# Tiles 0 and 1 centred first and scaled at their eviction, with the first statistics moved behind the low parts of the weights

## The chip, the cores and the metric

The kernel runs on one NeuronCore of one Trainium2 chip. The profile names five engines: PE (matrix multiplication; PEld is its loading of the stationary operand), DVE (the vector engine), ACT (the scalar engine), POOL (GpSimd) and SP, which here only issues DMAs. Each engine works through its own list of instructions in order, and waits on semaphores for the others. The metric is the device time of one execution in microseconds (us). Three runs of the kernel before gave 485.28, 485.30 and 487.21 us, a median of 485.3.

## The reference, cut to what matters

The input x has 2048 rows of 512 elements. Every row is normalised (mean taken off, divided by the root of its variance plus 1e-5). The result xn goes two ways: through q, k, v and a local dilated attention (32 heads of 16, a window of 8 keys at a distance of 2), and through a squared-ReLU network with 1792 hidden units. The product of the two is added to x.

```python
xn = _layernorm(x, axis=-1)            # (x - mean) / sqrt(var + 1e-5)
qkv = xn @ wqkv                        # 512 -> 3 * 512
# per position and head: softmax over 8 keys q.k / 4, then the weighted sum of v
s = attention(qkv) @ wo
h = xn @ w1 + b1
g = silu(relu(h)**2 @ w2 + b2)
return x + s * g
```

For a row with mean m and r = 1 / sqrt(var + 1e-5), xn @ w equals ((x - m) @ w) * r: the factor r may be applied to the row before the product or after it.

## The kernel before, in words

The 2048 rows are 16 tiles of 128 rows, and four chunks of four tiles. Precision is kept by splitting: each fp32 operand becomes a high part (ACT copies it to the type fp32r: `high`) and a low part (DVE or POOL takes the high part off the fp32 value: `low`; `split` does both), and a product is three matmuls, high by high, high by low and low by high (`PASSES`). A product of one tile with 512 columns is thus 12 matmuls of 128x512.

The work has two phases. In the first, q, k and v of all tiles are made and stored to DRAM (`sq`, `sk`, `sv`), from where the attention reads them back; tiles 2 to 15 go in pairs, most of them with a scheme that saves one product in eight by sums of the operands (the tiles `S`, made from `Sf`). In the second, the network runs chunk by chunk (`up`: 14 groups of 128 hidden units, PSUM tile `ph`; `down`: accumulated in `pb`), the attention on DVE runs beside it, and its result is multiplied by `wo` (`pw`). For chunk 0, `up` reads the transposed tiles 0 to 3 from one SBUF tile, `xT`; its first two groups are computed inside the last pair (a = 14) of the first phase.

Before a tile can be multiplied it goes through: a load of x (`load_x`), statistics on DVE (`stats`: BN_STATS, BN_AGGR into `mv`, and `rs` = variance + 1e-5), a power of -0.5 on POOL (`rs` again, in `moments`), the normalisation on DVE (`norm`: one TENSOR_SCALAR that subtracts the mean and multiplies by `rs`, into `xn`), a transpose on PE into PSUM (`pxT`), and the split into `xT` (`high` on ACT, `low` on DVE). The very first product, k of tile 0, takes no split: `x0` (`xT0f`) and the raw weights `wqraw` are multiplied in fp32, so that it can begin before the weights have been split. 18 transposes of the identity (`WARM`, tile `warm`) keep PE busy until then.

`evacuate` copies a product from PSUM into a staging tile `stg` (ACT, `AF.Copy`), and `store_qkv` sends a pair of tiles to DRAM through SP.

What sets the order: every compute call goes through `Ordered`, which keeps the order of the Python code on its engine; `queue` does the same for SP's DMAs. From pair 2 on, a table `plan` says behind which product (pair a, step 0 to 5) a function is called: `at(a, step, f, ...)`. Two running clocks, one of PE and one of DVE, add up an assumed price of each instruction and decide where the attention's instructions are put in; they are set to fixed values once (`clock.update`).

Of the kernel before, what the change touches and what calls it, by code (L numbers as in the profile page):

```python
# [9 lines left out]
F32 = mybir.dt.float32  # L10
FR = mybir.dt.float32r
AF = mybir.ActivationFunctionType
OP = mybir.AluOpType
AX = mybir.AxisListType

P = 128
S = 2048
D = 512
F = 1792
KT = D // P  # L20
# [11 lines left out]
GR = 8  # L32
# [11 lines left out]
SEVEN = range(4, 16, 2)  # L44
VSEVEN = range(6, 14, 2)

WARM = 18
WARM2 = 3

TURN = 4  # L50
# [9 lines left out]
def body(ctx: ExitStack, tc: tile.TileContext, x, wqkv, wo, w1, b1, w2, b2, out):  # L60
# [34 lines left out]
    PE, V, A, G = Ordered(nc.tensor, "PE"), Ordered(nc.vector, "V"), Ordered(nc.scalar), Ordered(nc.gpsimd)  # L95

    def not_before(t):
        clock["V"] = max(clock["V"], t)
# [3 lines left out]
    def queue(out, in_):  # L102

        tc.keep_in_program_order(dma(out, in_))

    const = ctx.enter_context(tc.tile_pool(name="const", bufs=1))
    dram = ctx.enter_context(tc.tile_pool(name="dram", bufs=1, space=bass.MemoryType.DRAM))
# [7 lines left out]
    def psA(name):  # L115
        return psum.tile([P, 512], F32, name=name, tag="acc", bufs=4)
# [4 lines left out]
    def psT(name):  # L121
        return psum.tile([P, 512], F32, name=name, tag="tp", bufs=2)
# [16 lines left out]
    xins = {}  # L139
# [3 lines left out]
    warm = psA("warm")  # L143
    for n in range(WARM):
        PE.transpose(warm[:, :P], ident, ident)
# [3 lines left out]
    def tile_rows(a, t):  # L149
        return a[t // 2 * UP:(t // 2 + 1) * UP, :].rearrange("(p e) d -> e p d", e=2)[t % 2]  # L150

    def load_x(t):
        xins[t] = px.tile([P, D], F32, name=f"x{t}", tag="x", bufs=4)
        queue(xins[t], tile_rows(x, t))
# [38 lines left out]
    mhalf = const.tile([P, 1], F32, name="mhalf")  # L193
# [3 lines left out]
    def constants():  # L197
# [5 lines left out]
        for w in range(W - 1):  # L203
            G.memset(mask[:GR, :(W - 1 - w) * DIL, w], -1e9)

    b1t = const.tile([P, NF], F32, name="b1t")
    b2t = const.tile([P, D], F32, name="b2t")

    sq = dram.tile([GR, S, CH], F32, name="sq")
    sk = dram.tile([GR, HALO + S, CH], F32, name="sk")  # L210
    sv = dram.tile([GR, HALO + S, CH], F32, name="sv")
# [15 lines left out]
    def load_u(what, u):  # L227
        n = BI if what == "q" else WIN
        src = dict(q=sq, k=sk, v=sv)[what]

        t = att.tile([P, n, CH], F32, name=f"{what}{u}", tag="k" if (what, u) == ("v", NU - 1) else what)
        row = src[0, u * UP:u * UP + 1, :]
        ap = bass.AP(tensor=row.tensor, offset=row.offset, ap=[[BI * CH, NB], [src.shape[1] * CH, GR], [1, n * CH]])
        A.dma_start(t.rearrange("p i c -> p (i c)"), ap)
        return t
# [20 lines left out]
    def start(n, u):  # L256
        tiles[n, u] = load_u(n, u)
        landing[n, u] = clock["PE"] + LOAD
# [161 lines left out]
    mv, means, rs, shifts, xn, xb, pTs, xt, xT, seen, Sf, Sp, xts = ({} for _ in range(13))  # L420

    def moments(t, st):
        mv[t] = px.tile([P, 2], F32, name=f"mv{t}", tag="mv", bufs=2)
        rs[t] = px.tile([P, 1], F32, name=f"rs{t}", tag="rs", bufs=4)
        V.bn_aggr(mv[t], st)
        V.tensor_scalar_add(rs[t], mv[t][:, 1:2], 1e-5)
        G.tensor_tensor(rs[t], rs[t], mhalf, op=OP.pow)
# [14 lines left out]
    def stats(t):  # L442
        st = px.tile([P, 6], F32, name=f"st{t}", tag="st", bufs=2)
        V.bn_stats(st, xins[t])
        moments(t, st)

    def norm(t):

        src = xins.pop(t)
        if t < TURN:  # L450
            xn[t] = dst = px.tile([P, 2, D], F32, name=f"xn{t}", tag="xb", bufs=2)[:, 0]
        else:
            if t % 2 == 0:
                xn[t] = px.tile([P, 4, 2, P], F32, name=f"xn{t}", tag="xn", bufs=2)
            dst = xn[t // 2 * 2][:, :, t % 2].rearrange("p a (k c) -> p k a c", k=KT)
            src = src.rearrange("p (k a c) -> p k a c", a=4, k=KT)
        if t < STATS:
            halves = [slice(0, D // 2), slice(D // 2, D)] if t == 0 else [slice(None)]
            for i in halves:
                V.tensor_scalar(dst[:, i], src[:, i], mv[t][:, 0:1], rs[t], op0=OP.subtract, op1=OP.mult)  # L460
        else:
            A.activation(dst, src, AF.Identity, bias=shifts.pop(t), scale=rs[t])
        if t < 2:
            load_x(t + 4)

    def place(t):
        if t < TPC:
            parts = xT[0][:, :, t]
        else:
            parts = xts[t] = pxT.tile([P, KT, 2, P], FR, name=f"xt{t}", tag="xt", bufs=4)  # L470
        xt[t] = parts.rearrange("p k a n -> p a k n")
# [95 lines left out]
    def qkv(t, s, between=None, late=False, new=True):  # L567

        ps = psA(f"pq{t}_{s}")
        order = [(kt, a, b) for kt in range(KT) for a, b in PASSES]  # L570
        if late:
            order.sort(key=lambda o: o[1])
        for n, (kt, a, b) in enumerate(order):
            PE.matmul(ps, xt[t][:, a, kt], wq[2 * s + kt // 2][:, b, kt % 2, :], start=n == 0, stop=n == 11,
                      skip_group_check=True)
            if between and n == 5:
                between()
        evacuate(t, s, ps, new)

    def evacuate(t, s, ps, new=True):  # L580
        if t % 2 == 0 and new:
            new_stg(t, s)
        A.activation(stgs[s][:, :, t % 2], ps.rearrange("p (g c) -> p g c", g=GR), AF.Copy)
        if t % 2:
            store_qkv(t, s)

# [42 lines left out]
    def highs(s, kt):  # L629
        for i in (kt, kt + 1):  # L630
            high(*wq_parts(s, i))

    def lows(s, kt):
        low(*wq_parts(s, kt), V)
        low(*wq_parts(s, kt + 1), V)


    stats(0)
    high(*wq_parts(1, 0))
    norm(0)  # L640
    xT[0] = xTa.tile([P, KT, TPC, 2, P], FR, name="xT0", tag="xT")
    place(0)
    pT = [psT(f"pxT0_{kt}") for kt in (0, 2)]
    for kt in range(KT):
        PE.transpose(pT[kt // 2][:, kt * P:(kt + 1) * P], xn[0][:, kt * P:(kt + 1) * P], ident)
    stats(1)
    low(*wq_parts(1, 0), V)

    x0 = hpool.tile([P, D], F32, name="xT0f", tag="h", bufs=4)
    for kt in (0, 2):  # L650
        cols = slice(kt * P, (kt + 2) * P)
        A.activation(x0[:, cols], pT[kt // 2][:, cols], AF.Copy)
    norm(1)
    for kt in range(1, KT):
        split(*wq_parts(1, kt), V)
    high(xt[0][:, 0], None, x0.rearrange("p (k n) -> p k n", k=KT))
    ps = psA("pq0_1")
# [7 lines left out]
    for kt in (0, 2):  # L665
        highs(0, kt)
    lows(0, 0)
    stats(2)
    clock.update(PE=12000.0, V=12500.0)
    qkv(1, 1, None, True)  # L670
    lows(0, 2)
    norm(2)
    stats(3)
    constants()
    qkv(0, 0, lambda: highs(2, 0))
    trans(2)
    lows(2, 0)
    norm(3)
    stats(4)
    qkv(1, 0, lambda: highs(2, 2))  # L680
    trans(3)
    lows(2, 2)
    stats(5)
    norm(4)
    norm(5)
    shuffle(4)
    lowx(2)
    lowx(3)

    next(stream)  # L690
    flush(clock["PE"] + 1000)
    qkv(0, 2)

    for d, x0, x1 in (((0, 0), (1, 0), (0, 0)), ((1, 0), (1, 2), (1, 0)),
                      ((1, 2), (1, 2), (0, 0)), ((0, 2), (0, 2), (1, 2))):
# [36 lines left out]
    def at(a, step, f, *args):  # L732
        if args[0] < NT:
            plan.setdefault((a, step), []).append((f, args))

    for a in range(2, NT, 2):
        n, t = {2: 2, 4: 1}.get(a, 0), a + 2
# [27 lines left out]
    for i in range(2):  # L765
        at(4, i, load_w, i)
    at(8, 1, lambda u: start("v", u), 0)
    plan.setdefault((10, 2), []).append((release, "k"))
    plan.setdefault((10, 4), []).append((release, "q"))

# [196 lines left out]
    for c in range(NCH):  # L967
# [7 lines left out]
        for f in range(2, NF):  # L975
# [74 lines left out]
        else:  # L1050
# [13 lines left out]
            for j in range(2, TPC):  # L1064
                n = D // 2 if j == TPC - 1 else D
# [25 lines left out]
```

## Time and profile before

| | |
|---|---|
| median of the three runs | 485.3 us |
| the profiled execution's own time | 485.13 us |
| its span, first to last instruction | 483.1 us |
| PE busy | 477.4 us (99% of the span) |
| DVE, ACT, POOL busy | 423.0, 240.0, 225.3 us |
| granted TensorE clock over the run | 1.00 |

The span leaves out what lies before the first and behind the last instruction, 2.0 us here. A row of a timeline gives the start, the duration, the engine, the line, the operation with output and inputs by tile name (numbers left out), shapes, a count where several were merged, and in brackets how long the engine sat idle before and what ended that. All compute instructions carry the line of the helper `call` (L91), so rows are told apart by tile names. Busy PE is not PE at its best: a transposed identity counts as busy too.

### The profile page before, as it was taken

Reading aid. Unit: us, or ns where it says so; the run is one execution under the profiler, and the core shown is the slowest. Engines: PE = TensorE matmul, PEld = TensorE weight load, DVE = VectorE, ACT = ScalarE, POOL = GpSimd, SP = SyncE. Lnnn points to the kernel's source line nnn. Section 1 sums busy time; section 2 is a strip of 40 time slices with the busy share of each in tenths; the row PEclk is TensorE's granted clock in tenths of the full one; section 3 lists DMA queues with packets and bytes.
Section 4 is the critical chain, followed back from the end, with each engine's and each line's share of the span. In section 5 each row is a group of like instructions: output and inputs, shape, how many; then the busy total and the mean of one; then the engine's idle time right before and its main releaser. Section 6 shows DMA issues by size and latency. Waiting matters only on the chain.

```text
span 483.1 us, 6128 instructions
## 1 busy us (share of the span) xinstructions
PE 477.4 (99%) x2190; PEld 396.6 (82%) x2190; DVE 423.0 (88%) x352; ACT 240.0 (50%) x441; POOL 225.3 (47%) x178
## 2 busy tenths in 40 slices
PE   8999999999999999999999999999999999999996
PEld 5888888888888888888888888888888888888885
DVE  5978999899499899999999999999999999889133
ACT  5548798856566565273513345342234543423240
POOL 1459853116986699436543322434433345253210
PEclk9999999999999999999999999999999999999999
DMA  7899999998779996571627548071707725220321
GB/s 283 243 251 258 277 243 302 263 306 269 209 198 228 255 224 151 178 166 43 170 72 185 115 164 190 26 189 43 197 16 196 224 48 145 43 86 27 87 105 71
DMA packets 71002, 81.47 MB, mean 169 GB/s; under 512 B 6204, under 2 KB 55612, under 8 KB 70972
## 3 DMA queue, kind: packets, MB, share of 16 engines
q1 hardware_dynamic: 65788, 54.87, 41.3%
q10 hardware_dynamic: 5184, 26.22, 21.8%
q8 instruction: 17, 0.28, 0.2%
q14 instruction: 13, 0.11, 0.1%
HBM read 50.60 MB, written 27.32 MB: 161 GB/s over the span
## 4 chain that ended last, share of the span: by engine, by line
PE 98%; DMA 1%; DVE 0%; POOL 0%; issue 0%; ACT 0%; POOLq 0%
PE ph L91 32%; PE pb L91 32%; PE pm L91 12%; PE pq L91 9%; PE pw L91 9%; PE pv L91 4%; DMA x<-in_A_x 1%; PE pxT L91 0%; DVE z L91 0%; DVE st L91 0%; POOL rs L91 0%; DVE xn L91 0%; ACT xT0f L91 0%; DVE mv L91 0%; DVE rs L91 0%
## 5 line engine op out<-in xcount | busy, mean ns | idle before, releaser
L91 PE MATMUL pb<-w,h 128*128 128x512 f32 x672 | 160.1, 389 | 0.0
L91 PEld LDWEIGHTS pb<-w,h 128*128 128x128 f32 x672 | 126.1, 188 | 26.2
L91 POOL TENSOR_TENSOR h<-hf,h 128x512 fp32r<-128x512 f32 x46 | 67.7, 1473 | 157.5 <-ACT hf L91 157.5
L91 PE MATMUL ph<-xU,w 128*128 128x512 f32 x504 | 120.2, 389 | 0.0
L91 ACT ACTIVATE ph<-ph,b1t 128x512 f32<-128x512 f32 x56 | 37.0, 661 | 153.9 <-PE ph L91 144.0
L91 PEld LDWEIGHTS ph<-xU,w 128*128 128x128 f32 x504 | 94.6, 188 | 19.6
L91 DVE TENSOR_TENSOR pr<-k,q 128x2048 f32<-128x2048 f32 x32 | 78.7, 2460 | 3.2 <-DMA q<-sq 2.5
L91 DVE TENSOR_TENSOR pv<-v,L 128x2048 f32<-128x2048 f32 x32 | 77.3, 2417 | 3.8 <-POOL L L91 3.1
L91 DVE TENSOR_REDUCE L<-pr 128x128 f32<-128x2048 f32 x32 | 73.0, 2281 | 0.7
L91 DVE TENSOR_REDUCE v<-pv 128x256 f32<-128x2048 f32 x32 | 72.9, 2279 | 0.7
L91 PE MATMUL pw<-wot,oT 128*128 128x512 f32 (+1 forms) x204 | 45.9, 376 | 0.0
L91 PEld LDWEIGHTS pw<-wot,oT 128*128 128x128 f32 x204 | 36.8, 188 | 7.1
L91 POOL TENSOR_TENSOR w<-w1r,w 128x512 fp32r<-128x512 f32 x14 | 31.6, 2259 | 23.4 <-ACT w L91 23.2
L91 PE MATMUL ph<-xT,w 128*128 128x512 f32 x168 | 40.0, 389 | 0.0
L91 PEld LDWEIGHTS ph<-xT,w 128*128 128x128 f32 x168 | 31.5, 188 | 6.6
L91 PE MATMUL pm<-wq,S 128*128 128x512 f32 x144 | 36.8, 392 | 0.0
L91 ACT ACTIVATE h<-ph 128x512 fp32r<-128x512 f32 x56 | 33.5, 599 | 1.8
L91 PE MATMUL pq<-wq,xT 128*128 128x512 f32 x132 | 30.9, 393 | 0.0
L91 PEld LDWEIGHTS pm<-wq,S 128*128 128x128 f32 x144 | 26.2, 188 | 5.3 <-DVE S L91 0.4
L91 PEld LDWEIGHTS pq<-wq,xT 128*128 128x128 f32 x132 | 24.5, 188 | 5.9 <-ACT xT L91 0.7
L91 ACT ACTIVATE hf<-ph 128x512 f32<-128x512 f32 x46 | 27.4, 595 | 1.9 <-POOL h L91 1.9
L91 PE MATMUL pm<-wq,xt 128*128 128x512 f32 x108 | 27.6, 392 | 0.0
(96 smaller groups left out, 531.0 us busy)
## 6 DMA issues: line engine op xcount, KB each, us to landing
k<-sk ACTq DMA_DIRECT2D x8, 960.0 KB, 7.1
v<-sv ACTq DMA_DIRECT2D x8, 960.0 KB, 7.4
sx<-xt SPq DMA_DIRECT2D x12, 512.0 KB, 5.8
xU<-sx ACTq DMA_DIRECT2D x12, 512.0 KB, 5.9
x<-in_A_x SPq DMA_DIRECT2D x16, 256.0 KB, 6.4
sk<-stg SPq DMA_DIRECT2D x8, 512.0 KB, 4.3
sq<-stg SPq DMA_DIRECT2D x8, 512.0 KB, 7.5
sv<-stg SPq DMA_DIRECT2D x8, 512.0 KB, 5.0
```

The costliest lines, as they stand in the source:

```text
L91: return tc.keep_in_program_order(f(*a, **k))
```

## The change

For tiles 0 and 1, `stats` and `norm` give way to two new functions. `centre` takes the statistics and at once subtracts the mean, without the factor; `deviation` then computes the factor `scales[:, t]` (one DVE addition and the power on POOL), which nothing on the way to the transposes needs any more. The factor is applied by `evacuate`: the ACT copy of the six products of tiles 0 and 1 (k, q and v of each) gets `scale=rs[t]`, one factor for each row.

The network still needs the normalised rows of these tiles, transposed, where the factor belongs to a column. So the two factors are written to DRAM and read back, repeated on all 128 partitions (`send_scales`, two DMAs on SP). In pair 10, `rescale` adds the two parts of `xT` of such a tile on POOL and multiplies by the factors (`full`, in a buffer of the x tiles); in pair 12, `rescaled` splits the result again into `xT` (ACT and POOL). That is six POOL instructions and two ACT instructions of 128x512.

Around it, the order of the start-up is changed: the statistics of tile 2 stand behind the low parts of the third and fourth block of q's weights (before them they stood in front), q of tile 1 comes before the transposes of tile 2, v of tile 0 before those of tile 3, the two statistics of tiles 4 and 5 follow the low parts of v's weights, and the low part of x tile 3 is made later in the code. The identity is transposed 16 times instead of 18.

```diff
-WARM = 18
+WARM = 16
...
+    def centre(t):
+        st = px.tile([P, 6], F32, name=f"st{t}", tag="st", bufs=2)
+        mv[t] = px.tile([P, 2], F32, name=f"mv{t}", tag="mv", bufs=2)
+        xn[t] = dst = px.tile([P, 2, D], F32, name=f"xn{t}", tag="xb", bufs=2)[:, 0]
+        src = xins.pop(t)
+        V.bn_stats(st, src)
+        V.bn_aggr(mv[t], st)
+        halves = [slice(0, D // 2), slice(D // 2, D)] if t == 0 else [slice(None)]
+        for i in halves:
+            V.tensor_scalar(dst[:, i], src[:, i], mv[t][:, 0:1], None, op0=OP.subtract)
+        load_x(t + 4)
+    def deviation(t):
+        rs[t] = scales[:, t:t + 1]
+        V.tensor_scalar_add(rs[t], mv[t][:, 1:2], 1e-5)
+        G.tensor_tensor(rs[t], rs[t], mhalf, op=OP.pow)
+    def send_scales(n):
+        if n == 0:
+            queue(rows_dram.rearrange("a p -> p a"), scales)
+        else:
+            queue(rows, rows_dram.rearrange("a p -> (a p)")[None, :].to_broadcast([P, 2 * P]))
+    def rescale(t):
+        fulls[t] = full = px.tile([P, KT, P], F32, name=f"full{t}", tag="x", bufs=4)
+        G.tensor_add(full, xt[t][:, 0].bitcast(F32), xt[t][:, 1].bitcast(F32))
+        G.tensor_mul(full, full, rows[:, None, t * P:(t + 1) * P].to_broadcast([P, KT, P]))
+    def rescaled(t):
+        split(xt[t][:, 0], xt[t][:, 1], fulls[t], G)
...
-        A.activation(stgs[s][:, :, t % 2], ps.rearrange("p (g c) -> p g c", g=GR), AF.Copy)
+        scale = dict(scale=rs[t]) if t < 2 else {}
+        A.activation(stgs[s][:, :, t % 2], ps.rearrange("p (g c) -> p g c", g=GR), AF.Copy, **scale)
...
-    stats(0)
+    centre(0)
     high(*wq_parts(1, 0))
-    norm(0)
+    deviation(0)
...
-    stats(1)
+    centre(1)
+    deviation(1)
     low(*wq_parts(1, 0), V)
...
-    norm(1)
     for kt in range(1, KT):
...
     lows(0, 0)
+    lows(0, 2)
     stats(2)
     clock.update(PE=12000.0, V=12500.0)
     qkv(1, 1, None, True)
-    lows(0, 2)
     norm(2)
     stats(3)
     constants()
     qkv(0, 0, lambda: highs(2, 0))
-    trans(2)
     lows(2, 0)
     norm(3)
+    qkv(1, 0, lambda: highs(2, 2))
+    trans(2)
+    lows(2, 2)
     stats(4)
-    qkv(1, 0, lambda: highs(2, 2))
-    trans(3)
-    lows(2, 2)
     stats(5)
...
     qkv(0, 2)
+    trans(3)
+    lowx(3)
...
+    for t in range(2):
+        at(6, 5 * t, send_scales, t)
+        at(10, 1 + 3 * t, rescale, t)
+        at(12, 3 + t, rescaled, t)
```

DVE at the start of the program, before (`st`, `mv`, `rs`, `xn` are a tile's statistics, mean and variance, factor and normalised rows, with the tile's number; `wq2`, `wq3` are k's split weights, `wq0`, `wq1` q's):

```order
L91 BN_AGGR mv0_157<-st0_155 128x2
L91 TENSOR_SCALAR rs0_158<-mv0_157 128x1
L91 TENSOR_SCALAR xn0_163<-x0_121,mv0_157,rs0_158 128x256 x2
L91 BN_STATS st1_175<-x1_125 128x6
L91 BN_AGGR mv1_177<-st1_175 128x2
L91 TENSOR_SCALAR rs1_178<-mv1_177 128x1
L91 TENSOR_TENSOR wq2_113<-wqraw1_0_123,wq2_113 128x512
L91 TENSOR_SCALAR xn1_186<-x1_125,mv1_177,rs1_178 128x512
L91 TENSOR_TENSOR wq2_113<-wqraw1_1_127,wq2_113 128x512
```

The same place with the change:

```order
L91 BN_AGGR mv0_157<-st0_156 128x2
L91 TENSOR_SCALAR xn0_158<-x0_119,mv0_157 128x256 x2
L91 TENSOR_SCALAR scales_144<-mv0_157 128x1
L91 BN_STATS st1_175<-x1_123 128x6
L91 BN_AGGR mv1_176<-st1_175 128x2
L91 TENSOR_SCALAR xn1_177<-x1_123,mv1_176 128x512
L91 TENSOR_SCALAR scales_144<-mv1_176 128x1
L91 TENSOR_TENSOR wq2_111<-wqraw1_0_121,wq2_111 128x512
L91 TENSOR_TENSOR wq2_111<-wqraw1_1_125,wq2_111 128x512
```

The rows `xn` no longer name `rs` among their inputs and stand ahead of the row that begins the factor; of tile 1 the centring now stands ahead of the low part of k's first weight block too.

DVE a little later, before, with the statistics of tile 2 between the halves of q's weights:

```order
L91 TENSOR_TENSOR wq0_111<-wqraw0_133,wq0_111 128x512 x2
L91 BN_STATS st2_218<-x2_136 128x6
L91 BN_AGGR mv2_220<-st2_218 128x2
L91 TENSOR_SCALAR rs2_221<-mv2_220 128x1
L91 TENSOR_TENSOR wq1_112<-wqraw0_133,wq1_112 128x512 x2
L91 TENSOR_SCALAR xn2_242<-x2_136,mv2_220,rs2_221 128x512
```

And with the change:

```order
L91 TENSOR_TENSOR wq0_109<-wqraw0_131,wq0_109 128x512 x2
L91 TENSOR_TENSOR wq1_110<-wqraw0_131,wq1_110 128x512 x2
L91 BN_STATS st2_219<-x2_134 128x6
L91 BN_AGGR mv2_221<-st2_219 128x2
L91 TENSOR_SCALAR rs2_222<-mv2_221 128x1
L91 TENSOR_SCALAR xn2_241<-x2_134,mv2_221,rs2_222 128x512
```

The low parts `wq1` come earlier by three instructions, and `xn2` now stands directly behind `rs2`, with nothing of DVE's own between them while POOL takes the power.

POOL in pairs 10 and 12 and at the head of pair 14, before (`stg` are staging sums, `w0` to `w2` the split weights of the network's groups):

```order
L91 TENSOR_TENSOR shift15_1028<-mean15_1026,rs15_1027 128x1
L91 TENSOR_TENSOR stg10_1_1086<-stg10_1_1086,stg10_0_1088 128x8x64
L91 TENSOR_TENSOR stg10_2_1087<-stg10_2_1087 128x4x64
L91 TENSOR_TENSOR w0_1320<-w1r0_593,w0_1320 128x512
L91 TENSOR_TENSOR w0_1320<-w2r0_594,w0_1320 128x512
L91 TENSOR_TENSOR stg12_1_1234<-stg12_1_1234,stg12_0_1236 128x8x64
L91 TENSOR_TENSOR stg12_2_1235<-stg12_2_1235 128x4x64
L91 TENSOR_TENSOR w1_1411<-w1r1_631,w1_1411 128x512
```

And with the change:

```order
L91 TENSOR_TENSOR full0_1150<-xT0_168 128x512
L91 TENSOR_TENSOR full0_1150<-full0_1150,rows_145 128x512
L91 TENSOR_TENSOR stg10_1_1087<-stg10_1_1087,stg10_0_1089 128x8x64
L91 TENSOR_TENSOR stg10_2_1088<-stg10_2_1088 128x4x64
L91 TENSOR_TENSOR full1_1217<-xT0_168 128x512
L91 TENSOR_TENSOR full1_1217<-full1_1217,rows_145 128x512
L91 TENSOR_TENSOR w0_1327<-w1r0_592,w0_1327 128x512
L91 TENSOR_TENSOR w0_1327<-w2r0_593,w0_1327 128x512
L91 TENSOR_TENSOR stg12_1_1241<-stg12_1_1241,stg12_0_1243 128x8x64
L91 TENSOR_TENSOR stg12_2_1242<-stg12_2_1242 128x4x64
L91 TENSOR_TENSOR xT0_168<-full0_1150,xT0_168 128x4x128
L91 TENSOR_TENSOR xT0_168<-full1_1217,xT0_168 128x4x128
```

The two `full` rows of tile 0 stand ahead of the sums of pair 10, those of tile 1 ahead of the split of `w0`, and the two low parts of `xT` ahead of the split of `w1`; all other rows keep their order.

More of the change, by code (lines that the diff above doesn't have):

```diff
@@ L204, in constants @@
             G.memset(mask[:GR, :(W - 1 - w) * DIL, w], -1e9)
+    scales = const.tile([P, 2], F32, name="scales")
+    rows = const.tile([P, 2 * P], F32, name="rows")
     b1t = const.tile([P, NF], F32, name="b1t")
     b2t = const.tile([P, D], F32, name="b2t")
+    rows_dram = dram.tile([2, P], F32, name="rows_dram")
     sq = dram.tile([GR, S, CH], F32, name="sq")
@@ L445, in stats @@
         moments(t, st)
+    def centre(t):
[18 more added lines that the diff above has]
+            queue(rows, rows_dram.rearrange("a p -> (a p)")[None, :].to_broadcast([P, 2 * P]))
+    fulls = {}
+    def rescale(t):
[4 more added lines that the diff above has]
+        split(xt[t][:, 0], xt[t][:, 1], fulls[t], G)
     def norm(t):
@@ L457, in norm @@
         if t < STATS:
-            halves = [slice(0, D // 2), slice(D // 2, D)] if t == 0 else [slice(None)]
-            for i in halves:
-                V.tensor_scalar(dst[:, i], src[:, i], mv[t][:, 0:1], rs[t], op0=OP.subtract, op1=OP.mult)
+            V.tensor_scalar(dst, src, mv[t][:, 0:1], rs[t], op0=OP.subtract, op1=OP.mult)
         else:
             A.activation(dst, src, AF.Identity, bias=shifts.pop(t), scale=rs[t])
-        if t < 2:
-            load_x(t + 4)
     def place(t):
@@ L687, in body @@
     lowx(2)
-    lowx(3)
     next(stream)
```

## The prediction

> **What bounds the kernel now.** I read the page first: how full each engine is, and which one the chain that ended last runs through.
>
> ```profile
> span 483.1 us, 6128 instructions
> PE 477.4 (99%) x2190; PEld 396.6 (82%) x2190; DVE 423.0 (88%) x352; ACT 240.0 (50%) x441; POOL 225.3 (47%) x178
> PE 98%; DMA 1%; DVE 0%; POOL 0%; issue 0%; ACT 0%; POOLq 0%
> ```
>
> PE is the bound from one end to the other, so time can only be won where PE is not busy with the problem. The table of busy time by stage says where that is.
>
> ```profile
> 0.00:10.71 10.71, 8.88 (x35) 5.86 (x35) 5.43 (x13) 5.62 (x9) 2.25 (x9) 1.00 0.76 269
> 20.00:85.00 65.00, 64.98 (x323) 54.89 (x322) 56.57 (x78) 48.71 (x107) 40.08 (x44) 1.00 1.00 262
> ```
>
> The columns are the stretch and its length, then busy time of PE, PEld, DVE, ACT and POOL. Behind 20 us PE has no holes; in the first 10.71 us it has 1.83 us of them, and much of its busy time is the transposed identity. The change works on this stretch, so I read its timeline, engine by engine: first how tile 0 becomes ready on DVE, then PE.
>
> ```profile
> 4.41 0.15 DVE L91 TENSOR_SCALAR rs<-mv 128x1 f32<-128x1 f32 x1
> 5.31 0.74 DVE L91 TENSOR_SCALAR xn<-x,mv,rs 128x256 f32<-128x256 f32 x2 [0.75 <-POOL rs L91]
> ```
>
> ```profile
> 1.35 4.10 PE L91 MATMUL warm<-ident 128*128 128x128 f32 x18 [1.35 <-POOL mhalf L91]
> 5.78 0.76 PE L91 MATMUL pxT<-ident,xn 128*128 128x128 f32 x4 [0.33 <-DVE xn L91]
> 6.70 2.84 PE L91 MATMUL pq<-wqraw,xT0f 128*128 128x512 f32 x6 [0.15 <-ACT xT0f L91]
> 9.39 0.63 PE L91 MATMUL pxT<-ident,xn 128*128 128x128 f32 x4
> 9.86 1.02 PE L91 MATMUL pq<-wqraw,xT0f 128*128 128x512 f32 x2
> 10.71 5.87 PE L91 MATMUL pq<-wq,xT 128*128 128x512 f32 x24
> ```
>
> DVE waits 0.75 us for POOL's power before it can normalise. PE's transposes wait for that (0.33), and the fp32 product of tile 0 for them: its first three weight blocks, two matmuls each, take 2.84 us, 0.95 a block. Then come the transposes of tile 1, the last fp32 block, and at 10.71 the split product of tile 1. Three more rows (ACT, DVE, PEld) tell what else is waited for.
>
> ```profile
> 7.21 1.98 ACT L91 ACTIVATE wq<-wqraw 128x512 fp32r<-128x512 f32 x3 [0.25 <-DMA wqraw<-in_A_wqkv]
> ```
>
> ```profile
> 7.48 0.15 DVE L91 TENSOR_SCALAR rs<-mv 128x1 f32<-128x1 f32 x1
> 7.56 0.69 DVE L91 TENSOR_TENSOR wq<-wqraw,wq 128x512 fp32r<-128x512 f32 x1
> 8.70 0.55 DVE L91 TENSOR_SCALAR xn<-x,mv,rs 128x512 f32<-128x512 f32 x1 [0.45 <-POOL rs L91]
> ```
>
> ```profile
> 15.14 0.99 PEld L91 LDWEIGHTS pq<-wq,xT 128*128 128x128 f32 x5 [0.23 <-DVE wq L91]
> ```
>
> ACT, idle, is released at 7.21 by the landing of the second block of k's weights: before that no engine has them. At 15.14 PE waits a little for the low parts of q's weights.
>
> **The change part by part, first the factor off the path.** Without it, centring starts where `rs` started: 4.41 instead of 5.31. Everything up to the first fp32 matmul moves by these 0.90 us, to 5.80. The 16 transposes of the identity, at 4.10/18 = 0.228 each, end at 5.00, when the first transposes could begin at 5.78 - 0.90 = 4.88: a fit, and those two removed cost nothing. But the 0.90 is not what is won. The first block now ends at 5.80 + 0.95 = 6.75, and the second needs weights that land at 7.2. It starts at about 7.24, where it started at 6.70 + 0.95 = 7.65 before: 0.41 us. The DMA is what is late next. The remainder keeps up: tile 1 is centred from 7.48 (where its `rs` stood), done by 8.03, and PE asks for it at 9.39 - 0.41 = 8.98. The bounds for this term: 0, were the transposes or ACT in the way, and 0.90, were the weights earlier; I take 0.41, by the row of their landing.
>
> **Low parts before the first statistics.** The statistics of tile 2 leave the front of `wq1`'s low parts. That ends the wait of 0.23 us at 15.14, of which the matmuls behind may have hidden part, so it is worth 0 to 0.23; I take 0.1, as the weight load runs ahead of the matmuls. The price is on DVE: `xn2` now follows `rs2` at once and DVE stands idle through POOL's power.
>
> ```profile
> 14.39 1.29 DVE L91 TENSOR_TENSOR wq<-wqraw,wq 128x512 fp32r<-128x512 f32 x2
> ...
> 17.07 1.29 DVE L91 TENSOR_TENSOR wq<-wqraw,wq 128x512 fp32r<-128x512 f32 x2
> ```
>
> The first of these was the cover; the wait is the 0.75 of the row at 5.31. Behind it in DVE's queue stand the low parts of v's weights: their first pair goes from 17.07 to 17.82, the second behind it with only `xn3` (0.55 as at 8.70) between, since the statistics of tile 4 have left: 17.82 + 1.29 + 0.55 = 19.66, the first of it done by 20.3. PE reads them in v of tile 0, which comes earlier:
>
> ```profile
> 19.60 0.60 PE L91 MATMUL pxT<-ident,xn 128*128 128x128 f32 x4
> 19.96 10.27 PE L91 MATMUL pq<-wq,xT 128*128 128x512 f32 x44
> ```
>
> It began at 19.96 behind the transposes of tile 3 and now begins ahead of them: 19.96 - 0.36 - 0.5 = 19.1. Its third block comes six matmuls of 10.27/44 = 0.233 later, at 20.5, the low part a matmul behind, at 20.7: a margin of 0.4. Without that cover the wait would cost up to 0.75. Also later by up to 0.75 is the low part of x tile 2, which stands further back on DVE; I count it as covered. The power of tile 3 on POOL slips by some 0.3 as well, and with it the zero fill that the first k load waits for on ACT's queue; ACT has no eviction due in that gap. Evictions with a factor for each row: six ACT copies of 0.60 like those before, off PE's path. The two orders of transposes and products on PE have the same instructions: nothing.
>
> **Does the lead last?** PE would run about 0.5 us ahead of the old time. In the first pairs it waits for DVE at one place only.
>
> ```profile
> 58.80 0.76 PEld L91 LDWEIGHTS pm<-wq,S 128*128 128x128 f32 x4 [0.44 <-DVE S L91]
> ```
>
> There DVE's low part of `S` is late by 0.44 for the weight load. The DVE chain behind it begins with an addition that waits for PE's product, so it moves with PE; were it tied to a landing of x instead, the whole 0.5 would be eaten here. Between -0.4 (the wait goes) and +0.5, I take 0.
>
> **The rescaling.** Two DMAs on SP, six POOL and two ACT instructions. SP first:
>
> ```profile
> 61.22 2.69 SPq L104 DMA_DIRECT2D sx<-xt  x2
> 67.63 2.51 SPq L104 DMA_DIRECT2D xb<-xn  x4
> ...
> 74.80 3.49 SPq L104 DMA_DIRECT2D sx<-xt  x2
> ```
>
> The write of the factors stands behind the first row: SP is idle from 63.9 to 67.6, which hides its issue. The read of them stands in front of the third, where SP is busy; it delays `sx` and the next `xb` by one issue, 0.4 to 1.3 us as these rows have it, and nothing but those transfers stands behind it. I take nothing. POOL, DVE and PE in pairs 10 to 14:
>
> ```profile
> 97.08 1.29 POOL L91 TENSOR_TENSOR stg<-stg,stg 128x512 f32<-128x512 f32 x1 [9.38 <-ACT stg L91]
> ...
> 116.97 1.19 POOL L91 TENSOR_TENSOR stg<-stg 128x256 f32<-128x256 f32 x1
> 120.17 3.07 POOL L91 TENSOR_TENSOR w<-w1r,w 128x512 fp32r<-128x512 f32 x1 [2.01 <-ACT w L91]
> ```
>
> ```profile
> 100.33 1.28 DVE L91 TENSOR_TENSOR S<-Sf,S 128x512 fp32r<-128x512 f32 x2
> ...
> 119.79 2.29 DVE L91 TENSOR_TENSOR pr<-k,q 128x2048 f32<-128x2048 f32 x1
> ...
> 133.77 0.69 DVE L91 TENSOR_TENSOR stg<-stg,pm 128x512 f32<-128x512 f32 x1 [7.03 <-PE pm L91]
> ```
>
> ```profile
> 102.51 1.52 PE L91 MATMUL pm<-wq,S 128*128 128x512 f32 x6
> ...
> 123.99 4.24 PE L91 MATMUL ph<-xT,w 128*128 128x512 f32 x18
> ```
>
> Tile 0's two instructions (2 x 1.29) fall into POOL's 9.38 us of idleness before 97.08, tile 1's into the one after 99.1. The two low parts start at 116.97 + 1.19 = 118.16 and end at 118.16 + 2 x 1.29 = 120.74; the idle 2.01 before 120.17 takes most of that. PE wants `xT`'s low part with the second matmul at 123.99 + 0.23, less the lead 123.7: a margin of 3.0.
>
> POOL and DVE do get in each other's way: the POOL row at 120.17 took 3.07 where its like takes 1.29, since it began inside DVE's `pr` (119.79 to 122.08) and ended 1.16 behind it. The Trainium skill, page "SBUF — State Buffer", section "SBUF: two separate sides", calls the pair of ports that VectorE and GpSimd share an exclusive lock, held for a whole instruction, and names VectorE instructions with two SBUF inputs. That rule speaks against the change; by it each added POOL instruction also holds up a DVE one, and the sum is that of the second rival below if the meetings fall badly. Here the two `S` low parts at 100.33 meet tile 1's `full`: by the rows one or two POOL instructions of 1.29 go first. The first `S` part, done at 101.0 before, is wanted by the third matmul at 102.51 + 0.45 - 0.5 = 102.5: still in time after one. All delay of DVE ends at 133.77, where it waited 7.03 us for PE. So I put the rescaling at 0; without this cover it would be six times 1.29, 7.7 us.
>
> **Sum.** 0.41 + 0.1 = 0.5 us off the profiled execution's 485.13 us (span 483.1 and 2.0 around it): 484.6. The median of the runs is 485.3, 0.2 above that execution, so 484.8 us.
>
> **The rivals.** First: nothing is won (about 485.3). The lead is lost at the `S` waits, or the second weight block is not what the fp32 product waits for. For it speaks the wait of 0.44 at 58.80; against it, that DVE's chain there starts from a PE product.
>
> Second, slower: the rescaling comes late at 123.99. It decides when the two low parts on POOL end behind 123.7. If both meet DVE's `pr` and take 3.07, they end at 124.3, 0.6 late; the first `S` part held up by two POOL instructions adds some 0.4. Without the lead's 0.5 being lost, that is +0.5, and with the longest POOL times twice, +1.1: 485.8 to 486.4. Against it: they start 1.6 us ahead of `pr`.
>
> Third, slower: PE's clock. The identity's transposes step by 0.228, the four at 9.39 by (9.86 - 9.39)/4 = 0.12: PE starts slow and turns fast between them. Real work now reaches further into that stretch. If it lasted through the first two weight blocks, they would take 2 x 1.9 from 5.8, to 9.6, where they ended at 8.6: +1.0, 486.3. Against it: PE is busy without a break from 1.35 to the first transposes, with a shorter pause than before behind it. The Trainium skill, page "TensorE: Matmul & The Clock Gate", Part 1, has the clock open after about 3.4 us of sustained activity, at a point that varies from run to run; by that rule 16 transposes (3.65 us) may just suffice or just not.
>
> Fourth, faster: all of 0.90 and both waits go, if the weights land earlier than the row of 7.21 tells: 484.1.
>
> **How the numbers follow.** Chances: my forecast (484.3 to 485.1) 0.60, nothing won 0.18, the late rescaling 0.13, the clock 0.05, the full gain 0.04. The likeliest gives 484.8. The range takes in the first rival and the bounds of the terms: down to 484.2 (0.41, 0.23 and 0.44 all won), up to 486.2 (most of the second rival). A change of 0.5% (2.4 us) is about what a measurement of this kernel can tell from none; no case reaches that by itself, so 0.94 is within it. I leave 0.04 for slower, where both slow rivals add up with a wait that I don't see, and 0.02 for faster.
>
> **What the changed profile would show.** Right: centring at 4.4, the first fp32 matmul near 5.8, then a hole in PE ended by the landing of `wqraw` near 7.2; the split product of tile 1 near 10.3 instead of 10.71; no wait for `wq` near 15; the first `ph` matmul 0.5 earlier, near 123.5, with no wait for POOL. Wrong: a wait of PE for `xT` from POOL there, a longer one for `S` near 42, 58 or 102, or slow matmuls behind 6 us. The forecast fails if the weights' landing itself moves, since the one large term hangs on it.

## The result, and the profile after

The changed kernel took 488.0 us in the median of 22 runs (486.3 to 493.5), the kernel before 485.3 beside it: a ratio of 1.0055, 95% interval 1.0034 to 1.0075 (the ratio goes by all runs, not by the two medians). It is slower by about half a percent, where 484.8 (484.2 to 486.2) had been forecast. The profiled execution took 487.41 us.

The page of the kernel after, in the lines that answer to those of before:

```profile
span 485.6 us, 6134 instructions
...
PE 479.6 (99%) x2188; PEld 395.9 (82%) x2188; DVE 422.6 (87%) x352; ACT 241.2 (50%) x443; POOL 247.4 (51%) x184
...
PE 70%; POOL 11%; DMA 7%; issue 7%; ACT 2%; DVE 1%; SPq 0%; POOLq 0%; ACTq 0%; DVEq 0%
```

The chain that ended last ran through PE for 98% of the span before. Now POOL, DMA and issue hold a quarter of it. The start-up is not where that comes from. PE's timeline of the first ten microseconds, and one row of its weight loads there:

```profile
4.82 0.86 PE L91 MATMUL pxT<-ident,xn 128*128 128x128 f32 x4
5.93 3.21 PE L91 MATMUL pq<-wqraw,xT0f 128*128 128x512 f32 x6 [0.26 <-ACT xT0f L91]
8.98 0.60 PE L91 MATMUL pxT<-ident,xn 128*128 128x128 f32 x4
9.41 1.02 PE L91 MATMUL pq<-wqraw,xT0f 128*128 128x512 f32 x2
10.26 0.97 PE L91 MATMUL pq<-wq,xT 128*128 128x512 f32 x3
```

```profile
7.15 0.30 PEld L91 LDWEIGHTS pq<-wqraw,xT0f 128*128 128x128 f32 x2 [0.93 <-DMA wqraw<-in_A_wqkv]
```

The fp32 product starts at 5.93, waits for the landing of the second weight block until 7.15, and the split product of tile 1 starts at 10.26 instead of 10.71. PE is ahead by 0.45 us.

To see where a lead is lost, each matmul's start after was set against the start of the same matmul before (negative: earlier than before, in us):

```
start before    58.8    83.7   90.9   103.2   117.9   135.1   174.5   180.0   185.4   last
difference     -0.53   -0.45  +0.34   +0.77   +1.32   +1.63   +1.91   +2.29   +2.65   +2.72
```

These are the seven longest waits of PE's weight loads from 90 us on (two answers of the timeline; what is in brackets is the wait):

```profile
90.86 1.22 PEld L91 LDWEIGHTS pm<-wq,S 128*128 128x128 f32 x6 [0.42 <-ACT pm L91]
103.62 0.76 PEld L91 LDWEIGHTS pm<-wq,S 128*128 128x128 f32 x4 [0.48 <-DVE S L91]
118.86 0.76 PEld L91 LDWEIGHTS pm<-wq,S 128*128 128x128 f32 x4 [0.69 <-DVE S L91]
136.39 1.23 PEld L91 LDWEIGHTS pm<-wq,xt 128*128 128x128 f32 x6 [0.42 <-ACT stg L91]
```

```profile
176.10 2.60 PEld L91 LDWEIGHTS ph<-xT,w 128*128 128x128 f32 x12 [0.35 <-DVE h L91]
...
181.93 2.59 PEld L91 LDWEIGHTS ph<-xT,w 128*128 128x128 f32 x12 [0.51 <-DVE h L91]
...
187.72 2.59 PEld L91 LDWEIGHTS ph<-xT,w 128*128 128x128 f32 x12 [0.48 <-DVE h L91]
```

The seven add up to 3.35 us, and the lead went from -0.53 to +2.72, by 3.25. The match is rough, since some shorter waits stand between them and the matmuls hide part of each. There are two losses: about 2 us between 84 and 140 us, where DVE and ACT are late, and 1 us between 174 and 188, where DVE's low parts of `h` are late.

**Where the first loss begins.** SP's queue, where the factors are written:

```profile
63.36 1.12 SPq L104 DMA_DIRECT2D rows_dram<-scales  x1
67.25 2.52 SPq L104 DMA_DIRECT2D xb<-xn  x4
...
71.01 0.38 SPq L104 DMA_DIRECT2D sk<-stg  x1
74.58 0.38 SPq L104 DMA_DIRECT2D sv<-stg  x1
```

The four `xb` are issued no later than before (67.25; 67.63 before). But DVE, which transposes them, waits. Its row before, and after:

```profile
73.37 1.32 DVE L91 STREAM_TRANSPOSE pxT<-xb 128x512 f32<-128x512 f32 x2 [0.18 <-DMA xb<-xn]
```

```profile
75.43 1.32 DVE L91 STREAM_TRANSPOSE pxT<-xb 128x512 f32<-128x512 f32 x2 [2.62 <-DMA xb<-xn]
```

`xb` had been just in time, and now lands 2 us late. SP's table of waits has a new row for the write (us in all, how often, the longest):

```profile
SPq L104 <- DMA rows_dram<-scales: 3.1, 1, 3.1
```

The store of `sv`, some transfers further on, could not be issued until the write of 1 KB had landed: SP was free at 71.01 + 0.38 = 71.4 and waited 3.1, to 74.5, 11 us after the write's issue. Between 70 and 74 us the other transfers are slow. The last two columns are the packets' time as a share of that of all DMA engines (above 1 where packets overlap), and GB/s; first before, then after:

```profile
70.00:74.00 4.00, 4.00 (x22) 3.41 (x21) 3.47 (x6) 3.94 (x11) 3.59 (x7) 1.00 1.07 207
```

```profile
70.00:74.00 4.00, 4.00 (x23) 3.42 (x22) 2.68 (x5) 3.59 (x9) 3.59 (x7) 1.00 1.24 69
```

The engines have packets all the time, and a third of the bytes move.

**Where the second loss begins.** Another pair of rows, of ACT's timeline:

```profile
146.97 0.52 ACTq L91 DMA_DIRECT2D k<-sk  x1
...
156.32 0.52 ACTq L91 DMA_DIRECT2D q<-sq  x1
156.95 0.66 ACT L91 ACTIVATE ph<-ph,b1t 128x512 f32<-128x512 f32 x1 [7.84 <-DMA w2r<-in_B_w]
```

ACT stood for 7.84 us, since the load of `q` in its queue waited for the landing of a `w2r` (the raw weights of a group for the network's second product). DVE, which takes `ph` from ACT, stood with it, and from here on its low parts of `h` are late:

```profile
158.82 0.69 DVE L91 TENSOR_TENSOR h<-ph,h 128x512 fp32r<-128x512 f32 x1 [3.98 <-ACT ph L91]
```

That `w2r` was issued by SP at 148.11, behind the load of `k` (960 KB); before, it was issued at 144.13, ahead of it. SP issues it when POOL has made the low part of an earlier weight. That row of POOL, and the row of DVE beside it, before and then after:

```profile
142.81 1.29 POOL L91 TENSOR_TENSOR w<-w2r,w 128x512 fp32r<-128x512 f32 x1
143.27 2.98 DVE L91 TENSOR_TENSOR pv<-v,L 128x2048 f32<-128x2048 f32 x1
```

```profile
144.19 2.73 DVE L91 TENSOR_TENSOR pv<-v,L 128x2048 f32<-128x2048 f32 x1
144.73 3.35 POOL L91 TENSOR_TENSOR w<-w2r,w 128x512 fp32r<-128x512 f32 x1
```

Before, POOL's row began first and took 1.29. After, DVE's began first, POOL's took 3.35 and ended at 148.08. It began 1.92 us later than before, little more than the 1.65 by which PE itself was behind there; the 2.06 that put the `w2r` behind the load of `k` are the meeting with DVE. What had changed on POOL are the two low parts of `xT`, ahead of the weight splits:

```profile
119.36 3.00 POOL L91 TENSOR_TENSOR xT<-full,xT 128x512 fp32r<-128x512 f32 x2
122.33 3.33 POOL L91 TENSOR_TENSOR w<-w1r,w 128x512 fp32r<-128x512 f32 x1
```

The `w` row began at 120.17 before, so the weight splits behind it meet DVE's instructions at other places. How this turns the meeting at 144 us round was not followed step by step; the runs below show in which kernels it is turned round.

### The profile page after: what moved, and what is told of

Same layout as the page of the kernel before. It is cut to its first block, busy times and chain, and to the rows that moved or that the text cites. A ratio compares the mean times of both kernels' runs of the same rounds, so it can differ in the third digit from the quotient of the medians.

```text
span 485.6 us, 6134 instructions
## 1 busy us (share of the span) xinstructions
PE 479.6 (99%) x2188; PEld 395.9 (82%) x2188; DVE 422.6 (87%) x352; ACT 241.2 (50%) x443; POOL 247.4 (51%) x184
## 4 chain that ended last, share of the span: by engine, by line
PE 70%; POOL 11%; DMA 7%; issue 7%; ACT 2%; DVE 1%; SPq 0%; POOLq 0%; ACTq 0%; DVEq 0%
PE pb L91 26%; PE ph L91 25%; PE pw L91 9%; PE pq L91 8%; POOL w L91 5%; DMA sv<-stg 3%; DMA w2r<-in_B_w 2%; POOL stg L91 2%; PE pm L91 2%; POOL full L91 1%; DMA wqraw<-in_A_wqkv 1%; ACT stg L91 1%; POOL rs L91 1%; ACT waste L91 1%; POOL xT L91 1%
## 5 line engine op out<-in xcount | busy, mean ns | idle before, releaser
L91 POOL TENSOR_TENSOR h<-hf,h 128x512 fp32r<-128x512 f32 x46 | 76.6, 1665 | 145.6 <-ACT hf L91 143.1
L91 DVE TENSOR_TENSOR pr<-k,q 128x2048 f32<-128x2048 f32 x32 | 79.7, 2490 | 0.8
L91 POOL TENSOR_TENSOR w<-w2r,w 128x512 fp32r<-128x512 f32 x14 | 28.4, 2025 | 0.0
```

Of the source, the lines that this page charges most:

```text
L91: return tc.keep_in_program_order(f(*a, **k))
```

## The experiments

The theory after this reading: the DMAs of the factors hold up the transfers behind them (first loss), and the two low parts of `xT` make POOL late (second loss); the start-up's gain is real. The rivals: POOL's six instructions carry all of it through the port that they share with DVE; or the new start-up does. "Before" is the kernel before on the same chip, times are medians of 12 runs, and ratios, with their 95% intervals, go by all runs and can differ by 0.1 to 0.2% from the quotient of two medians. The runs without the DMAs or without the rescaling leave out the factor for the network, which then sees tiles 0 and 1 centred but not scaled.

### Taking the change apart

Without the two DMAs:

```diff
-        at(6, 5 * t, send_scales, t)
+        G.memset(rows, 1.0)        # in constants()
```

> The two DMAs of the factors are left out, and rows is filled with ones at the start, so the network sees tiles 0 and 1 centred but not scaled; the POOL and ACT work of the rescaling stays. Theory A (the DMAs stall the transfers behind them, so that the xb tiles land 2 us late and DVE falls behind; POOL's six instructions cost something of their own only where the low parts of xT push the loads of w2r behind the load of k, about 1 us at 176 to 188): most of the loss goes; 485.0 to 486.0, DVE's waits for xb near 73 and 89 back at 0.2 and 0.5 us. Theory B (POOL's six instructions of 1.3 to 1.5 us, which share a port with DVE, carry the loss): 487 to 488, S late at 90, 103 and 118 as before.

Without the rescaling:

```diff
-        at(10, 1 + 3 * t, rescale, t)
-        at(12, 3 + t, rescaled, t)
```

> The two DMAs stay; the POOL and ACT work of the rescaling is left out, so the network sees tiles 0 and 1 centred but not scaled. Theory A: xb still lands 2 to 3 us late, PE still loses 1 to 2 us between 83 and 140; 486.0 to 487.5, with a wide spread. Theory B: 484.7, the start-up's gain alone.

Without both:

```diff
-    for t in range(2):
-        at(6, 5 * t, send_scales, t)
-        at(10, 1 + 3 * t, rescale, t)
-        at(12, 3 + t, rescaled, t)
```

> Neither DMAs nor rescaling: the start-up and the scaled evictions alone (the network sees tiles 0 and 1 centred but not scaled). Theory A and theory B both: the lead of 0.5 to 0.6 us that PE has at 42 us lasts to the end, 484.6 to 484.9. Theory C (the new order of the start-up or the lead itself causes the later waits): 486 to 488.

With the write alone:

```diff
-    for t in range(2):
-        at(6, 5 * t, send_scales, t)
-        at(10, 1 + 3 * t, rescale, t)
-        at(12, 3 + t, rescaled, t)
+    at(6, 0, send_scales, 0)
```

> As the run without the rescaling, and without the read of the factors too: of the added DMAs only the write of 256 single numbers of 4 bytes is left. Theory A1 (the write is what stalls the transfers: packets of 1 KB that took 3 us behind it): xb late by 2 us near 73 and SP waiting for the write, 486 to 487. Theory A2 (the read, which repeats the factors on 128 partitions, is what delays): 484.7, no late xb near 73.

| what is left of the change | us | ratio to before (485.53) |
|---|---|---|
| start-up, rescaling (no DMAs) | 485.64 | 1.0003 (0.9991 to 1.0014) |
| start-up, both DMAs | 486.57 | 1.0020 (1.0004 to 1.0036) |
| start-up alone | 484.73 | 0.9976 (0.9962 to 0.9991) |
| start-up, the write alone | 486.2 | 1.0003 (0.9984 to 1.0022) |

(One of the 12 runs with the write alone took 1138 us, for no reason that I know; the ratio leaves it out, and without it the median is 486.0.) The start-up alone gave 484.73, what the prediction had for the whole change: the third theory falls. The rescaling costs 485.64 - 484.73 = 0.9 us, the DMAs 486.57 - 484.73 = 1.8, and 1.3 to 1.4 of that is the write. The two add up to 2.7 of the 3.3 between 484.7 and 488.0; the remaining 0.6 is little more than the scatter of such medians, and was not followed. POOL's work alone does not carry the loss, so the first rival, by which it carries all of it, falls as well. The traces put the write's loss where the theory has it: matmul by matmul against before, PE loses 1.83 us between 80 and 120 us with both DMAs, 1.25 with the write alone, and nothing in the start-up alone. In the run with the write alone the rows of the stall are back (SP's wait, DVE's wait, the stretch from 70 to 74 us):

```profile
SPq L104 <- DMA rows_dram<-scales: 3.2, 1, 3.2
```

```profile
75.33 1.32 DVE L91 STREAM_TRANSPOSE pxT<-xb 128x512 f32<-128x512 f32 x2 [2.92 <-DMA xb<-xn]
```

```profile
70.00:74.00 4.00, 4.00 (x24) 3.48 (x23) 2.30 (x4) 3.59 (x10) 3.59 (x7) 1.00 1.29 81
```

And in the run without DMAs, where POOL's work is left, ACT's wait is there without any stall of the transfers, and so is the meeting (POOL's row took 3.37, from 142.06, inside DVE's from 141.53):

```profile
144.38 0.52 ACTq L91 DMA_DIRECT2D k<-sk  x1
...
153.61 0.52 ACTq L91 DMA_DIRECT2D q<-sq  x1
154.24 0.66 ACT L91 ACTIVATE ph<-ph,b1t 128x512 f32<-128x512 f32 x1 [7.77 <-DMA w2r<-in_B_w]
```

There PE loses 1.7 us between 150 and 195, more than the 0.9 of the medians, in an execution that had won 1.0 at the start.

### What it is in the write, and what in the rescaling

The low parts earlier, in the kernel without DMAs:

```diff
-        at(12, 3 + t, rescaled, t)
+        at(12, t, rescaled, t)
```

> As the run without the DMAs (rows filled with ones, so tiles 0 and 1 reach the network unscaled), but the two low parts of xT are made three steps earlier, at the head of pair 12, where POOL is idle for ten microseconds, and no longer in front of the split of w1. Theory A2 (what the rescaling cost there, 0.9 us, came from POOL being late at 144, so that the load of w2r was issued behind the load of k, landed late, and ACT stood for 7.8 us behind the load of q): w2r is issued ahead of k again, ACT's wait of 7.8 us is gone, and the time is that without rescaling, 484.7 to 484.9. Rival (POOL's six instructions cost by sharing a port with DVE, wherever they are): 485.5 to 486.

The write spread out, in the kernel with the write alone:

```diff
-    rows_dram = dram.tile([2, P], F32, name="rows_dram")
+    rows_dram = dram.tile([2, P, 16], F32, name="rows_dram")
-            queue(rows_dram.rearrange("a p -> p a"), scales)
+            queue(rows_dram[:, :, 0].rearrange("a p -> p a"), scales)
```

> As the run with the write alone, but the 256 numbers go to places 64 bytes apart in DRAM instead of 4 bytes apart; still 256 packets of 4 bytes. If neighbouring numbers in one place of DRAM hold each other up: no packets of 3 us, xb not late near 73, 484.7 to 485.0. If it is the 256 small packets as such: like the write alone, 486, SP waiting 3 us for the landing.

The write packed (`scales` has 64 columns, with the factors in columns 0 and 32, the others zeroed on POOL in `constants`):

```diff
-            queue(rows_dram.rearrange("a p -> p a"), scales)
+            V.transpose(out=rows[:, 0:64], in_=scales)
+            queue(rows_dram.rearrange("a (b c) -> b a c", c=32),
+                  rows[:, 0:64].rearrange("(b r) (a c) -> b r a c", r=32, c=32)[:, 0])
```

> As the run with the write alone, but DVE turns the factors first (one transpose of 128x64), so that the same 1 KB goes to DRAM as 8 packets of 128 bytes. Theory A1 (the small packets stall the transfers behind them): the stall is gone, xb near 73 in time, 484.7 to 485.0. Rival (any write at this place in SP's order holds the transfers up, whatever its size): 486.

Before took 485.74 beside these. With the low parts earlier: 485.1 (0.9986, 0.9975 to 0.9998), where it had been 485.64; it lies between the two expectations, nearer to the first. POOL's row takes 1.29 again (143.05), ahead of DVE's (143.50). ACT's long wait is gone, since `w2r` goes out at 144.37 and the load of `k` behind it:

```profile
145.59 0.52 ACTq L91 DMA_DIRECT2D k<-sk  x1
147.51 0.52 ACTq L91 DMA_DIRECT2D q<-sq  x1
```

Of the 14 profiles here that row of POOL takes over 3 us in two, the kernel after and the run without DMAs, and ACT stands long for a `w2r` in the same two.

With the numbers 64 bytes apart: 484.63 (0.9973, 0.9960 to 0.9986), the time without any write. They are as many packets of 4 bytes as before, and the stretch from 70 to 74 us moves 213 GB/s, as the start-up alone does:

```profile
70.00:74.00 4.00, 4.00 (x23) 3.41 (x23) 3.63 (x7) 3.94 (x11) 3.60 (x6) 1.00 1.02 213
```

So it is neither the number of the packets nor their size that stalls the other transfers, but that they are written side by side in DRAM (of distances, 64 bytes alone was tried). Why side by side is slow, no run here shows. The packed write has no stall either (DVE's wait for `xb` near 73 is gone), yet it took 485.68 (0.9990, 0.9975 to 1.0005), 0.7 over the expectation. In its profile PE loses 1.4 us between 42 and 47, ahead of the write, at waits for `S`, behind a first `xb` that came later still than in the other runs with the new start-up (DVE waits 4.77 for it at 35.14). The zeroing among POOL's work ahead of that is no sure reason: the first run of the next section has it too and loses 0.2 us there, and the run with the low parts earlier has none and loses 0.8.

### The start-up's order, and a version without these losses

The whole change with the packed write and the low parts earlier, first with the read of the factors where it was, then with the read behind `xb` of pair 12 and the zeroing at the head of POOL's list:

> The whole change with two things altered: the factors are written as 8 packets of 128 bytes, and the two low parts of xT are made at the head of pair 12. Theory A with both its parts: the two losses of about 1.8 and 0.9 us go but for what the read of the factors costs (0 to 0.5 us): 484.7 to 485.3, under the kernel before. If the read costs as much as the write did: 486 to 487.

```diff
-        at(6, 5 * t, send_scales, t)
+        at((6, 8)[t], 2 * t, send_scales, t)
```

> The whole change, with the factors written as 8 packets of 128 bytes, the zeroing that this needs put to the very start of POOL's list, the read of the factors three products later (behind xb of pair 12, where SP is idle), and the two low parts of xT at the head of pair 12. If the write, the place of the read and the place of the low parts are all that the change lost by: 484.7 to 485.0, below the kernel before, and no late xb at 73 or 89. If the read costs wherever it is: 485.5 to 486.

They took 486.01 (1.0006, 0.9990 to 1.0022) and 485.52 (0.9990, 0.9969 to 1.0012): better than the change by 2 to 2.5 us, and no better than before. Both expectations were missed, by 0.7 and by 0.5 to 0.8, and both times lie where the expectations put a read that costs. The profiles do not bear that out for the read alone. With the late read PE loses 1.1 us between 42 and 47, ahead of the read, then 0.35 between 80 and 120, where DVE still waits 0.89 for `xb` at 90, and 0.56 at waits for `h` at 180 and 185. With the early read PE loses 1.36 at one wait for `S` at 118.35 (1.48): DVE comes to it behind an `xb` for which it waited 1.48 at 90.40 (0.45 in the start-up alone), and behind rows that took 0.96 and 1.56 beside POOL's rescaling instead of 0.42. What of these losses is the read of 128 KB and what the rescaling was not taken apart. Whether the new order of the start-up has a part in it is told by the next pair, both without DMAs and rescaling, run beside the second of these:

```diff
-    lows(0, 2)
     stats(2)
...
+    lows(0, 2)                     # behind qkv(1, 1), and so on: the order of the kernel before
```

> As the run with neither DMAs nor rescaling (tiles 0 and 1 reach the network unscaled), but the start-up behind the first product in the order of the kernel before: statistics of tile 2 ahead of the low parts of wq1, transposes of tiles 2 and 3 where they were, statistics of 4 and 5 too. So only centring and scaled evictions differ from the kernel before. By the prediction's terms 0.41 of the gain stays and 0.1 goes: 484.8 to 484.9, PE waiting some 0.2 us for wq near 14.7. Rival (the reordering carries more, since it delays xn4 and the first xb near 33 us): time 484.3 to 484.6, S in time at 43.

> The run with neither DMAs nor rescaling once more, on the chip of the two beside it, as what they are compared with: 484.7.

Centring with the old order: 484.68 (0.9971, 0.9953 to 0.9990); with the new order: 484.84 (0.9964, 0.9945 to 0.9983). The new order is worth nothing that these runs can tell. It does end the wait for `wq`, but the first `xb` comes later, and PE pays for it at waits for `S`: in the eleven profiles with the new order it loses 0.2 to 0.3 us between 42 and 47 in seven and 0.7 to 1.4 in four, those in which DVE waited over 4 us for that `xb`; in the two with the old order it loses nothing there. The row of DVE with the new order, then with the old:

```profile
33.71 1.32 DVE L91 STREAM_TRANSPOSE pxT<-xb 128x512 f32<-128x512 f32 x2 [4.08 <-DMA xb<-xn]
```

```profile
31.79 1.31 DVE L91 STREAM_TRANSPOSE pxT<-xb 128x512 f32<-128x512 f32 x2
```

Last, the whole computation with the old order, the low parts earlier, and no DMAs for the factors at all:

```diff
+        A.activation(rows[:, :P], ident, AF.Identity, bias=rs[0], scale=0.0)
+        A.activation(rows[:, P:], ident, AF.Identity, bias=rs[1], scale=0.0)
...
+        turned = psH("turned")
+        for t in range(2):
+            PE.transpose(turned[:, t * P:(t + 1) * P], rows[:, t * P:(t + 1) * P], ident)
+        A.activation(rows, turned[:, :2 * P], AF.Copy)
```

> The whole computation again, without the two DMAs: ACT spreads each factor along its row, PE turns the two squares by two transposes behind q of tile 0, ACT copies them to rows; the start-up is in the order of the kernel before and the low parts of xT are made at the head of pair 12. Theory A (the change lost by the write of the factors, by their read and by the place of the low parts, and by nothing else): the run with centring alone, 484.7, and 2 x 0.12 us for the transposes on PE, 484.9 to 485.1, below the kernel before. If the rescaling on POOL costs more than the run with ones in rows showed (485.1 against 484.7): 485.5 to 486.

It took 484.95 beside 485.65 (0.9984, 0.9972 to 0.9996), as expected, and faster than both kernels by a little: by 0.7 us, where the centring alone had gained 1.0 on another chip. The difference would be two transposes and the rescaling.

## Why the prediction was wrong

**Right: the factor off the path.** Centring at 4.36 (4.41 forecast), the fp32 product at 5.93 (5.80), its second block at 7.15 with the landing (7.24), the split product of tile 1 at 10.26 (10.3). The 0.41 of this term measured 0.45 at 10.7. That it came so close in one execution is partly luck, since the landing moves: in the 13 profiles with centring the second block began between 6.63 and 7.62, and the split product of tile 1 between 9.68 and 10.73, with 10.33 in the middle. The two runs of the start-up alone, 484.73 and 484.84, lie on the sum of 484.8 (beside a kernel before of 485.5 and 485.7 there, so the gain was 0.8 and not 0.5). From 42 to 59 us the lead of the profiled execution was kept (0.55 and 0.53), as forecast.

**Half right: low parts before the first statistics.** The wait at 15.14 went. The price was put down as covered, with the margins in v of tile 0, which held; the work of tile 4, further back in the same queue, was not followed. The first `xb` came 1.5 to 2 us later, PE had to wait for `S` at 43 us, one of the prediction's own signs of being wrong, and the term is worth 0 in the medians and not 0.1.

**Wrong, the step that failed most: "The write of the factors ... SP is idle from 63.9 to 67.6, which hides its issue"** and the sentence on the read. The issue was hidden, as said: `xb` went out on time. But a DMA was priced by its issue on the queue alone. Its packets and its landing were left out, and the landing is what SP's later transfers and DVE wait for. The sentence on the read, that "nothing but those transfers stands behind it", named `xb` and did not ask when it is needed. For the `xb` behind the write the row of before at 73.37, which ends with 0.18 of waiting for it, would have said it: a margin of nothing. The two DMAs cost 1.8 us and not 0.

**Wrong: "So I put the rescaling at 0".** What was looked at behind the low parts of `xT` was the first `ph` product, and it did not wait for them. What was missed stands behind them on POOL itself: the splits of the weights, by which SP may load the next ones. They have slack until the load of `k` overtakes one of the loads. That came about where one split began inside a DVE instruction, 25 us behind the low parts, and took 3.35 us instead of 1.29; from there it costs 0.9 us. The prediction knew such meetings (3.07 instead of 1.29) but looked for them up to the first `ph` product only. The second rival had the place (POOL's low parts, 1.1 us at most) but not the path, and the cover named for DVE's delays, the 7.03 us of idleness at 133.77, lies ahead of the place where it was lost.

The Trainium skill, page "SBUF — State Buffer", section "SBUF: two separate sides", has POOL and DVE lock each other out for whole instructions. By it each added POOL instruction can hold up a DVE one, or be held up, wherever it stands. The traces agree that the two do: in the run with the low parts earlier DVE's two low parts of `S` at 100.44 took 2.38 us beside POOL's `full` (1.28 before), and in the kernel after POOL's row at 144.73 took 3.35. But this costs time only where somebody waits for it. With the low parts moved PE lost 0.1 us behind 80 us, and the time was 485.1, 0.4 above the start-up alone, with intervals that overlap. The one meeting that changed the order of two loads cost 0.9.

The Trainium skill, page "DMA: Bandwidth & Descriptors", section "Why small descriptors are slow (HBM only)", gives overheads for each packet and each descriptor. The run with 256 packets of 4 bytes at 64 bytes' distance lost nothing, so the trace does not bear these out as the reason for this stall.

The clock's rival did not happen: the granted clock is 1.00 and the second fp32 block, from 7.16 to 8.12, takes 0.96 us, as the first did before. The chance for slower by over 0.5% was 0.04, and the measured 0.55% fell there, since two terms with a price of 0 were wrong in the same direction.

## What to carry to other kernels

Price an added DMA by three things: its issue, the transfers that run beside it, and who waits, directly or by the order of the queue, for its landing; then read the margin of the next transfer's consumer from its own row. A write of single numbers side by side in DRAM can hold up the other transfers for microseconds, as it did here: transpose them on chip first, or keep them on chip. When work is put on an engine with idle time, follow its queue to the next thing that another engine's DMA waits for, not only to the consumer of the added work. Where two engines hold each other up, a small shift can change which of them goes first, far behind the added work.

## What was not expected of the hardware

1 KB, written as 256 numbers of 4 bytes next to each other in DRAM, landed 11 us after its issue and cut the traffic of all 16 DMA engines from 207 to 69 GB/s for 4 us; the same numbers 64 bytes apart left it at 213. Packets of 1 KB between 62 and 76 us took up to 3.6 us, and up to 0.2 before and with the numbers apart. An ACT copy with a factor for each row took 690 ns where the plain one took 596, as the groups of the kernel after tell (count, then busy time and mean), off the path here:

```profile
L91 ACT ACTIVATE stg<-pq 128x512 f32<-128x512 f32 x10 | 6.0, 596 | 8.0 <-PE pq L91 7.9
L91 ACT ACTIVATE stg<-pq,scales 128x512 f32<-128x512 f32 x6 | 4.1, 690 | 6.4 <-PE pq L91 6.3
```
